# Direct products issued by high and low terms, each with its own wait, in an order planned from the engines' first moments

## The chip, the cores and the metric

The kernel runs on one core of a Trainium2 chip. The core has a matrix engine (PE in the profile, with its weight loads shown apart as PEld), two engines for elementwise work (DVE and ACT), a fourth that is hardly used here (POOL), and queues that issue DMA transfers (SP's, and a few on ACT). The metric is the device time of one launch in microseconds. Of the kernel before, three runs gave 1079.13, 1081.22 and 1082.68 us.

## The reference, cut to what matters

```
# attention in chunks of 32 queries; window 16 left, 8 right, and 8 memory slots
scores = 0.125 * q_c @ k_full.T ; a = softmax(scores) ; out = a @ v_full
x = out, as 3072 tokens x 512
# first expert layer
h = x @ w_in ; r = max(h, 0) ; g = s * r*r + b ; x1 = g @ w_out       # 512 -> 2048 -> 512
# second expert layer
h = x1 @ w_in2 ; g = h * sigmoid(1.702 * h) ; y = g @ w_out2
```

All inputs and the output are float32. (The weights w_in and w_out reach the kernel as raw 64-bit words, which it turns into float32 itself.)

## The kernel before, in words

**Two ways of multiplying.** Every operand of a large product is split into a high and a low part (a float32r value, and the rest), and three terms are computed: high times high, high weight times low data, low weight times high data. In the trace the parts of weights are `wih`/`wil` (w_in) and `woh`/`wol` (w_out), those of the tokens `xh`/`xl`, those of the gated middle layer `gh`/`gl`. The first four of the six blocks of 512 tokens go through the first layer as *direct products* (`step`, lines 630 to 632 and 668): `ph` is one 128-row slice of h, and `accA`, `accB` gather the four slices of the result. All the rest, from about 438 us on, are products of a Winograd-like scheme with seven pieces (`wino`, lines 998 to 1004 and 1153): there one sum is copied by ACT from one PSUM bank to another (line 1046), and further products are added onto the copy.

**Units.** A unit of direct work is one slice of 128 of the 2048 middle features, for a block of 512 tokens: 12 matmuls into `ph` (4 slices of the model width, 3 terms), then relu, square, scale and shift, then a cast to `gh` and a subtraction to `gl`, then 12 matmuls into `accA` and `accB`. The first two slices are done in two halves of 256 tokens (A: tiles 0 and 1; Z: tiles 2 and 3), so that direct work can begin before the whole block has been through the attention.

**Attention.** Tiles of 128 tokens, singly for tiles 0 to 3 and then in pairs. PE computes the scores `sc` (line 441), DVE the maximum and the subtraction, ACT the exponent (line 466), PE turns the result (`pp`, line 474), ACT or DVE copy it (`px`), PE multiplies with the values (`o`, line 502), DVE divides (line 507), PE turns it back (`xx`, line 516), and ACT or DVE cast `xh` (line 238) and DVE subtracts `xl` (line 533). The buffers for keys, queries and values hold two tiles, so the loads for tiles 2 and 3 are issued when the work on tiles 0 and 1 has let go of them. Weights are read by DMA into `st`, put together by two ACT and three DVE instructions, and split.

**The planner.** The order of everything is fixed when the program is built. Each piece of work is an operation of class `Plan` with a time by which it is wanted, the engines that could do it with a duration for each, and what it waits for. `order` places the operations one by one: the earliest start wins, among near ones the earliest due; a DMA ends a constant after its bytes have passed a single shared pipe; an operation on another engine is ready 0.15 us after what it waits for. All engines begin at time 0. A DMA's constant is 1.0 us for issues up to 12 us and 2.2 us later. Each engine then executes its list strictly in that order; an instruction that is not ready holds up all behind it.

**Fillers.** Where the plan leaves PE without work for more than 0.3 us before the fourth operation of `plan.first` (the first accumulating products), it puts in matmuls on a tile of zeros (`idle<-cold`, line 1291), one for every 0.24 us of the gap, and ten more at the very start (`warm<-cold`, line 288). Each float32 filler is two passes in the trace.

**What the change touches.** `WARM`; the constants of `Plan`, the line with the free times in `order`, and the two lines that turn gaps into fillers; in `step` the functions `hid` (four operations of 3 matmuls, all of which wait for every high and low part) and `out_part` (four operations of 3 matmuls, all of which wait for `gh`, `gl`, `woh` and `wol`), and the operations made of them.

Of the kernel before, what the change touches and what calls it, by code (L numbers as in the profile page):

```python
# [32 lines left out]
WARM = 10  # L33
# [15 lines left out]
class Plan:  # L49


    DMA_START, DMA_END, DMA_LATER = 1.1, 1.0, 2.2
    BEAT = 0.24

# [19 lines left out]
    def order(self):  # L74
# [7 lines left out]
        free = {"pe": 0.0, "act": 0.0, "dve": 0.0, "pool": 0.0, "sp": 0.0, "aq": 0.0, "none": 0.0}  # L82
# [53 lines left out]
        while left:  # L136
# [29 lines left out]
            if e in ("sp", "aq"):  # L166
# [5 lines left out]
                ends[i] = dma_free + (self.DMA_LATER if t > 12.0 else self.DMA_END)  # L172
# [32 lines left out]
def attention_moe_moe(ctx: ExitStack, tc: tile.TileContext, q_t, k_w, v_w, w_in1, w_out1, s_b, w_in2, w_out2, out):  # L205
# [409 lines left out]
    def step(i):  # L615
# [7 lines left out]
        def hid(k):  # L623
            def fn(e):
                if k == 0:
                    T["ph", i] = ps_h.tile([P, 512], F32, tag="h", name="ph")[:, :r.stop - r.start]
                wh, wl = [w[:, k * P:(k + 1) * P] for w in T[win]]
                xh, xl = [x[:, k, r] for x in T["x", m, b]]
                ph = T["ph", i]
# [28 lines left out]
        def out_part(k):  # L658
            def fn(e):
                if fresh and k % 2 == 0:  # L660
                    T["acc", group, k // 2] = pair(halves[k // 2], halves[k // 2])
                a = T["acc", group, k // 2][:, k % 2]
                wh, wl = T[wout]
                gh, gl = T["g", i]
                s = slice(k * P, k * P + P)
                terms = ((a[:, r], wh[:, s], gh), (a[:, r], wh[:, s], gl), (a[:, r], wl[:, s], gh))
                for x, (o, lt, rh) in enumerate(terms):
                    nc.tensor.matmul(o, lt, rh, start=fresh and x == 0, stop=(done and x == 2))  # L668
            return fn

        dur = 0.68 * n + (0.0 if n == 1 else 0.03)
        d = None
        uses = [("h", i)]
        ready = list(o_w[win])
        for x in {0: range(2), 256: range(2, 4)}[r.start] if r != ALL else range(4):
            ready += o_x[4 * b + x]
# [673 lines left out]
```

## Time and profile before

| | |
|---|---|
| runs | 1081.22 us (median of 1079.13, 1081.22, 1082.68) |
| profiled execution | 1080.21 us, of which the span from first to last instruction is 1078.2 us |
| PE | 1061.2 us busy, 8653 matmuls |
| DVE, ACT | 760.0 us and 603.8 us busy |
| DMA | 265.68 MB, 246 GB/s on average |

A row of a timeline gives the start and the length of a piece of work in us, the engine, the source line, the operation, what it writes and reads, its shape, how many instructions were merged into the row, and in brackets how long the engine had been idle and what ended that. The ends of matmuls are modelled and overlap the next one's start, so times between matmuls are read from start to start: a matmul of 128x512 takes 0.39 us by its length, and the next one starts 0.23 us after it.

### The profile page before, as it was taken

To read this page: it belongs to the slowest core of one execution; us is meant where nothing else is said; L and a number is where in the kernel's file an instruction comes from. 1 tells how busy PE (TensorE), PEld (TensorE's weight loads), DVE (VectorE), ACT (ScalarE), POOL (GpSimd) and SP (SyncE) were. 2 spreads that over 40 slices of the span, in tenths; PEclk is the share of its full clock that TensorE was granted. 3 is DMA by queue.
4 is the path that set the end of the run, shared out by engine and by line. 5 is a ranking of instruction groups with operands and counts; after the bars stand their busy time and mean duration, and the time that the engine had idled before them with its cause. 6 is when DMAs were issued, how large, how long until landed. Compare 5 with 4: busy or idle time off the path is not lost.

```text
span 1078.2 us, 21826 instructions
## 1 busy us (share of the span) xinstructions
PE 1061.2 (98%) x8653; PEld 915.4 (85%) x8653; DVE 760.0 (70%) x1146; ACT 603.8 (56%) x929; POOL 0.7 (0%) x6
## 2 busy tenths in 40 slices
PE   8999999999999999999999999999999999999998
PEld 8878888888888788777888787999888999888998
DVE  6899895777888678878899466995224985222954
ACT  4777755555666566678744566553455542454432
POOL 0000000000000000000000000000000000000000
PEclk9999999999999999999999999999999999999999
DMA  9898843667699985979878889867666766656662
GB/s 349 284 321 292 263 136 129 230 210 233 226 344 330 318 292 186 314 247 312 305 220 295 299 304 334 301 221 254 195 190 201 235 207 213 196 188 207 196 199 79
DMA packets 151541, 265.68 MB, mean 246 GB/s; under 512 B 14224, under 2 KB 65424, under 8 KB 151440
## 3 DMA queue, kind: packets, MB, share of 16 engines
q1 hardware_dynamic: 151152, 263.77, 73.7%
q8 instruction: 68, 1.11, 0.4%
q10 hardware_dynamic: 288, 0.52, 0.1%
q14 instruction: 33, 0.27, 0.1%
HBM read 190.84 MB, written 73.40 MB: 245 GB/s over the span
## 4 chain that ended last, share of the span: by engine, by line
PE 94%; DMA 2%; ACT 2%; DVE 1%; issue 1%; DVEq 0%; SPq 0%; ACTq 0%
PE pc L1153 10%; PE accA L668 8%; PE accB L668 7%; PE pd L1153 6%; PE pb L1153 6%; PE ph L630 6%; PE ph L632 5%; PE ph L631 5%; PE pc L1159 3%; PE pd L1002 3%; PE pd L1004 3%; PE pd L1003 3%; PE ph L1002 3%; PE ph L1003 3%; PE ph L1004 3%; PE pb L1002 2%
## 5 line engine op out<-in xcount | busy, mean ns | idle before, releaser
L1127 DVE TENSOR_TENSOR oj<-G,oj 128x1024 fp32r<-128x1024 f32 x72 | 87.9, 1223 | 54.4 <-ACT oj L1124 53.7
L1124 ACT CAST oj<-G 128x1024 fp32r<-128x1024 f32 x72 | 75.6, 1051 | 87.7 <-PE pd L1153 28.9
L637 ACT ACTIVATE r<-ph 128x512 f32<-128x512 f32 (+1 forms) x66 | 38.6, 585 | 68.9 <-PE ph L632 60.0
L1124 ACT CAST oq<-G 128x1024 fp32r<-128x1024 f32 x40 | 42.1, 1052 | 48.2 <-PE pc L1153 20.0
L1127 DVE TENSOR_TENSOR oq<-G,oq 128x1024 fp32r<-128x1024 f32 x40 | 48.9, 1223 | 27.8 <-ACT oq L1124 27.6
L1153 PE MATMUL pc<-wih,oj 128*128 128x256 f32 x336 | 62.4, 283 | 0.0
L1136 DVE TENSOR_TENSOR G<-G 128x1024 f32<-128x1024 f32 x48 | 57.4, 1219 | 0.2
L652 ACT CAST gh<-r 128x512 fp32r<-128x512 f32 (+1 forms) x66 | 40.1, 607 | 31.3 <-PE accB L668 27.0
L656 DVE TENSOR_TENSOR gl<-r,gh 128x512 fp32r<-128x512 f32 (+1 forms) x66 | 44.2, 669 | 18.1 <-ACT gh L652 17.8
L1014 ACT ACTIVATE G<-ys 128x512 f32<-128x512 f32 x64 | 40.5, 633 | 24.0 <-DVE ys L1056 24.0
L630 PE MATMUL ph<-xh,wih 128*128 128x512 f32 (+1 forms) x136 | 53.8, 396 | 0.0
L1153 PE MATMUL pd<-wih,oj 128*128 128x256 f32 x288 | 53.8, 283 | 0.0
L1153 PEld LDWEIGHTS pc<-wih,oj 128*128 128x128 f32 x336 | 53.3, 192 | 0.0
L631 PE MATMUL ph<-xl,wih 128*128 128x512 f32 (+1 forms) x136 | 52.2, 384 | 0.3 <-DVE xl L533 0.3
L632 PE MATMUL ph<-xh,wil 128*128 128x512 f32 (+1 forms) x136 | 52.0, 383 | 0.3 <-DVE wil L333 0.3
L668 PE MATMUL accA<-gl,woh 128*128 128x512 f32 (+1 forms) x132 | 51.1, 387 | 1.0 <-DVE gl L656 1.0
L668 PE MATMUL accA<-gh,woh 128*128 128x512 f32 (+1 forms) x132 | 51.3, 389 | 0.0
L668 PE MATMUL accB<-gh,woh 128*128 128x512 f32 (+1 forms) x132 | 51.1, 387 | 0.0
L668 PE MATMUL accA<-gh,wol 128*128 128x512 f32 (+1 forms) x132 | 50.7, 384 | 0.0
L668 PE MATMUL accB<-gl,woh 128*128 128x512 f32 (+1 forms) x132 | 50.5, 383 | 0.2 <-issue 0.2
L355 ACT ACTIVATE u<-st 128x512 f32<-128x512 f32 x64 | 43.0, 673 | 13.7 <-DMA st<-w_in 11.0
L668 PE MATMUL accB<-gh,wol 128*128 128x512 f32 (+1 forms) x132 | 50.6, 383 | 0.0
(253 smaller groups left out, 3111.3 us busy)
## 6 DMA issues: line engine op xcount, KB each, us to landing
wih<-wodh SPq DMA_DIRECT2D x112, 256.0 KB, 3.2
wil<-wodl SPq DMA_DIRECT2D x112, 256.0 KB, 3.7
wih<-wch SPq DMA_DIRECT2D x96, 256.0 KB, 3.7
wil<-wcl SPq DMA_DIRECT2D x96, 256.0 KB, 4.0
st<-w_in SPq DMA_DIRECT2D x32, 512.0 KB, 5.6
st<-w_out SPq DMA_DIRECT2D x32, 512.0 KB, 5.9
k<-k_w SPq DMA_DIRECT2D x24, 512.0 KB, 6.5
v<-v_w SPq DMA_DIRECT2D x24, 512.0 KB, 6.1
```

What stands on the lines that cost most here:

```text
L630: nc.tensor.matmul(ph, wh, xh, start=(k == 0), stop=False)
L631: nc.tensor.matmul(ph, wh, xl, start=False, stop=False)
L632: nc.tensor.matmul(ph, wl, xh, start=False, stop=(k == KT - 1))
L656: nc.vector.tensor_tensor(out=gl, in0=T["r", i], in1=gh.bitcast(F32), op=ALU.subtract)
L668: nc.tensor.matmul(o, lt, rh, start=fresh and x == 0, stop=(done and x == 2))
L1002: nc.tensor.matmul(ph, wh, xh, start=first and i == 0, stop=False, skip_group_check=True)
L1003: nc.tensor.matmul(ph, wh, xl, start=False, stop=False, skip_group_check=True)
L1004: nc.tensor.matmul(ph, wl, xh, start=False, stop=i == 1, skip_group_check=True)
L1124: nc.scalar.copy(out=T[kh], in_=g_of(ty, z))
L1127: nc.vector.tensor_tensor(out=T[kl], in0=g_of(ty, z), in1=T[kh].bitcast(F32), op=ALU.subtract)
L1136: o_raw[out, x] = [op(need, {"dve": 1.22}, lambda e: nc.vector.tensor_tensor(out=g_of(out, z), in0=g_of(a, z), in1=g_of(b, z), op=o), afte ...
L1153: nc.tensor.matmul(a, lt[:, z], rh, start=first and t % 2 == 0 and x == 0, stop=p == HALF - 1 and x == 2, skip_group_check=True)
```

## The change

It replaces the four operations of three terms by three operations of one term each: for `ph` first high times high for all four slices of the width, which waits only for the high weight and the high tokens; then high weight times low tokens, waiting for the low tokens; then low weight times high tokens, waiting for the low weight. The planner may put either of the last two first, and other work between them. The products into `accA` and `accB` are split likewise (high times `gh`, which waits for `gh` and `woh`; then those with `gl` and with `wol`), except in the last unit of a block, which stays as it was. The number and the shapes of the matmuls are the same.

The planner's engines now begin at 0.7 to 1.0 us, each DMA ends 2.2 us after its bytes, a gap becomes fillers only for what is over 0.3 us of it, the warming matmuls are 8, and the fillers end at the first accumulating operation, not at the fourth.

```diff
-WARM = 10
+WARM = 8
...
-    DMA_START, DMA_END, DMA_LATER = 1.1, 1.0, 2.2
+    DMA_START, DMA_END = 1.1, 2.2
     BEAT = 0.24
+    BEGIN = {"pe": 1.0, "act": 0.7, "dve": 0.8, "pool": 0.7, "sp": 0.7, "aq": 0.7, "none": 0.0}
...
-        free = {"pe": 0.0, "act": 0.0, "dve": 0.0, "pool": 0.0, "sp": 0.0, "aq": 0.0, "none": 0.0}
+        free = dict(self.BEGIN)
...
-                ends[i] = dma_free + (self.DMA_LATER if t > 12.0 else self.DMA_END)
+                ends[i] = dma_free + self.DMA_END
...
                 if idle > 0.3:
-                    full.append((None, int(idle / self.BEAT)))
+                    full.append((None, int((idle - 0.3) / self.BEAT)))
...
-        def hid(k):
-            def fn(e):
-                if k == 0:
+        def hid(x, y):
+            def fn(e):
+                if not seen_["hid"]:
                     T["ph", i] = ps_h.tile([P, 512], F32, tag="h", name="ph")[:, :r.stop - r.start]
...
-                nc.tensor.matmul(ph, wh, xh, start=(k == 0), stop=False)
-                nc.tensor.matmul(ph, wh, xl, start=False, stop=False)
-                nc.tensor.matmul(ph, wl, xh, start=False, stop=(k == KT - 1))
+                for k in range(KT):
+                    seen_["hid"] += 1
+                    nc.tensor.matmul(T["ph", i], T[win][x][:, k * P:(k + 1) * P], T["x", m, b][y][:, k, r],
+                                     start=seen_["hid"] == 1, stop=seen_["hid"] == 3 * KT)
...
-        for k in range(KT):
-            after = list(ready)
-            if d is not None:
-                after.append(d)
-            d = op(at_h[i], {"pe": dur}, hid(k), after=after, alloc=[("h", ("h", i))] if k == 0 else [],
-                   uses=[("x", m, b), win])
+        wh, wl = o_w[win]
+        high, low = [x[0] for x in tokens], [x[1] for x in tokens]
+        d = op(at_h[i], {"pe": third}, hid(0, 0), after=[wh] + high, alloc=[("h", ("h", i))], uses=[("x", m, b), win])
+        ds = [op(at_h[i], {"pe": third}, hid(0, 1), after=[d] + low, uses=[("x", m, b), win]),
+              op(at_h[i], {"pe": third}, hid(1, 0), after=[d, wl], uses=[("x", m, b), win])]
...
-            if fresh and not plan.first[3:]:
-                plan.first.append(d)
...
+        if done:
+            ds = []
+            for k in range(KT):
+                ds.append(op(at_o[i], {"pe": dur}, out_part((k,), ((0, 0), (0, 1), (1, 0))), after=[g1, g2, wh, wl] + prev + ds[-1:],
...
+        else:
+            d = op(at_o[i], {"pe": third}, out_part(range(KT), ((0, 0),)), after=[g1, wh] + prev, alloc=taken, uses=[("g", i), wout])
+            ds = [op(at_o[i], {"pe": third}, out_part(range(KT), ((0, 1),)), after=[d, g2], uses=[("g", i), wout]),
+                  op(at_o[i], {"pe": third}, out_part(range(KT), ((1, 0),)), after=[d, wl], uses=[("g", i), wout])]
+            if fresh and not plan.first:
+                plan.first += [d]
```

The plan made from this differs from the plan before over the first half of the program; the last 2665 matmuls stand in the same order. (Line numbers of the changed kernel are higher by one, and `ph` and the accumulators have one line each, 632 and 665.) Three places on PE:

**The way to the first direct product.** PE before, from the attention of tiles 0 and 1 to the first direct product of half A. Ahead of these rows stand 1 filler, 10 warming matmuls, the scores of tile 0, 9 fillers, the scores of tile 1 and the first turn.

```order
L1291 MATMUL idle<-cold 128x128 x3
L502 MATMUL o<-v,px 32x64 x32
L1291 MATMUL idle<-cold 128x128 x8
L474 MATMUL pp<-ident,qe 128x128 x4
L516 MATMUL xx<-ident,px 128x128 x4
L1291 MATMUL idle<-cold 128x128
L502 MATMUL o<-v,px 32x64 x32
L1291 MATMUL idle<-cold 128x128 x6
L516 MATMUL xx<-ident,px 128x128 x4
L1291 MATMUL idle<-cold 128x128 x9
L630 MATMUL ph<-xh_351,wih 128x256
L631 MATMUL ph<-xl_352,wih 128x256
```

The same place now. Ahead of it stand 3 fillers, 8 warming matmuls, 5 fillers, the scores of tile 0, 10 fillers, the scores of tile 1 and the first turn.

```order
L1292 MATMUL idle<-cold 128x128 x2
L503 MATMUL o<-v,px 32x64 x32
L1292 MATMUL idle<-cold 128x128 x5
L475 MATMUL pp<-ident,qe 128x128 x4
L517 MATMUL xx<-ident,px 128x128 x4
L503 MATMUL o<-v,px 32x64 x32
L1292 MATMUL idle<-cold 128x128 x4
L517 MATMUL xx<-ident,px 128x128 x4
L1292 MATMUL idle<-cold 128x128 x2
L632 MATMUL ph<-xh_353,wih 128x256 x4
L632 MATMUL ph<-xh_353,wil 128x256 x4
L632 MATMUL ph<-xl_354,wih 128x256 x4
```

From the scores of tile 0 to the first direct product stand 36 fillers before and 23 now, and ahead of those scores 11 fillers and warming matmuls before and 16 now; the four products with the low tokens come last.

**The last pair of attention tiles.** PE before, from the scores of the last pair of tiles on; `ph` belongs to a unit of the fourth block.

```order
L441 MATMUL sc<-k,qe 32x64 x64
L630 MATMUL ph<-xh_3311,wih 128x512
L631 MATMUL ph<-xl_3312,wih 128x512
L632 MATMUL ph<-xh_3311,wil 128x512
L630 MATMUL ph<-xh_3311,wih 128x512
L631 MATMUL ph<-xl_3312,wih 128x512
L632 MATMUL ph<-xh_3311,wil 128x512
L630 MATMUL ph<-xh_3311,wih 128x512
L631 MATMUL ph<-xl_3312,wih 128x512
L632 MATMUL ph<-xh_3311,wil 128x512
L630 MATMUL ph<-xh_3311,wih 128x512
L631 MATMUL ph<-xl_3312,wih 128x512
```

PE now, from the same scores on.

```order
L442 MATMUL sc<-k,qe 32x64 x64
L632 MATMUL ph<-xh_3313,wih 128x512 x4
L665 MATMUL accA<-gh,woh 128x512 x2
L665 MATMUL accB<-gh,woh 128x512 x2
L665 MATMUL accA<-gl,woh 128x512 x2
L665 MATMUL accB<-gl,woh 128x512 x2
L665 MATMUL accA<-gh,wol 128x512 x2
L665 MATMUL accB<-gh,wol 128x512 x2
L665 MATMUL accA<-gh,woh 128x512 x2
L665 MATMUL accB<-gh,woh 128x512 x2
L665 MATMUL accA<-gl,woh 128x512 x2
L665 MATMUL accB<-gl,woh 128x512 x2
```

The turn `pp` of that pair came after 12 matmuls of 128x512; now 48 of them stand between the scores and it.

**A product onto a copied sum.** PE before, some 40 us into the Winograd part: the last of the products A of a piece into `ph`, and those that follow into the bank `pb`, whose other half takes ACT's copy of that sum.

```order
L1003 MATMUL ph<-xh_5202,wih 128x512
L1004 MATMUL ph<-xh_5202,wil 128x512
L1002 MATMUL pb<-xl_5508,wih 128x512
L1003 MATMUL pb<-xl_5508,wih 128x512
L1004 MATMUL pb<-xl_5508,wil 128x512
L1002 MATMUL pb<-xl_5508,wih 128x512
L1003 MATMUL pb<-xl_5508,wih 128x512
L1004 MATMUL pb<-xl_5508,wil 128x512
```

PE now, after the same products into `ph`.

```order
L1004 MATMUL ph<-xh_5199,wih 128x512
L1005 MATMUL ph<-xh_5199,wil 128x512
L1003 MATMUL pc<-wzh,wih 128x512
L1004 MATMUL pc<-wzl,wih 128x512
L1005 MATMUL pc<-wzh,wil 128x512
L1003 MATMUL pc<-wzh,wih 128x512
L1004 MATMUL pc<-wzl,wih 128x512
L1005 MATMUL pc<-wzh,wil 128x512
L1003 MATMUL pd<-wzh,wih 128x512
L1004 MATMUL pd<-wzl,wih 128x512
```

Twelve other products (into `pc` and `pd`) now stand between the sum and the first product into `pb`. At two more places of that part, where `pd` followed twelve products into `pc` at once, six products into `pd` from other operands now stand in between.

On ACT, at the passage from direct to Winograd products, the copies of the four finished sums (`y<-accA` twice, `y<-accB` twice) and one cast `sx<-sx` of 128x1024 now stand ahead of the cast of `xh` that the second group of Winograd products waits for; before, DVE did that cast, after one such copy.

## Rows read from the trace of the kernel before

**Rows 1.** The page: PE's busy time, and the chain that ended last.

```profile
PE 1061.2 (98%) x8653; PEld 915.4 (85%) x8653; DVE 760.0 (70%) x1146; ACT 603.8 (56%) x929; POOL 0.7 (0%) x6
...
PE 94%; DMA 2%; ACT 2%; DVE 1%; issue 1%; DVEq 0%; SPq 0%; ACTq 0%
```

**Rows 2.** Waits of PE: who waited for whom; us in total, times, longest.

```profile
PE xx L516 <- DVE px L507: 1.5, 1, 1.5
PE pd L1002 <- ACT pd L1046: 1.3, 2, 0.7
```

**Rows 3.** Busy time by stretch: PE, PEld, DVE, ACT, POOL (instructions); PEclk; DMA.

```profile
36.00:39.00 3.00, 2.94 (x14) 2.95 (x15) 2.99 (x7) 0.76 (x2) 0.00 (x0) 0.50 0.95 285
39.40:42.40 3.00, 3.00 (x28) 3.00 (x27) 2.35 (x6) 2.85 (x7) 0.00 (x0) 1.00 0.72 200
442.10:445.50 3.40, 3.40 (x9) 2.68 (x9) 3.40 (x8) 1.14 (x3) 0.00 (x0) 0.50 0.90 288
60.00:100.00 40.00, 39.13 (x539) 31.10 (x538) 36.03 (x63) 32.09 (x56) 0.00 (x0) 1.00 0.91 325
```

**Rows 4.** Timeline of PE, 0 to 43 us.

```profile
1.64 4.10 PE L288 MATMUL warm<-cold 128*128 128x128 f32 x20
5.67 0.86 PE L441 MATMUL sc<-k,qe 64*32 64x64 f32 x64
6.46 2.27 PE L1291 MATMUL idle<-cold 128*128 128x128 f32 x18
...
12.40 0.42 PE L502 MATMUL o<-v,px 64*32 64x64 f32 x21 [0.71 <-issue]
...
20.87 0.36 PE L630 MATMUL ph<-xh,wih 128*128 128x256 f32 x1
...
25.13 0.63 PE L441 MATMUL sc<-k,qe 64*32 64x64 f32 x36 [0.85 <-issue]
...
34.02 0.63 PE L516 MATMUL xx<-ident,px 128*128 128x128 f32 x4 [1.48 <-DVE px L507]
...
36.06 0.58 PE L631 MATMUL ph<-xl,wih 128*128 128x256 f32 x1 [0.31 <-DVE xl L533]
...
42.51 0.40 PE L630 MATMUL ph<-xh,wih 128*128 128x512 f32 x1
```

**Rows 5.** Timeline of DVE around 33 us.

```profile
32.58 0.69 DVE L238 CAST xh<-xx 128x512 fp32r<-128x512 f32 x1 [0.56 <-PE xx L516]
33.19 0.68 DVE L507 TENSOR_TENSOR px<-o,den 128x512 f32<-128x512 f32 x1
```

**Rows 6.** DMA issues from 15.2 to 16.2 us: KB each, median us to landing.

```profile
qe<-q_t SPq DMA_DIRECT2D x2, 256.0 KB, 6.2
```

**Rows 7.** Timeline of PE around the last pair of attention tiles.

```profile
357.88 1.51 PE L441 MATMUL sc<-k,qe 64*32 64x64 f32 x128
...
363.30 0.88 PE L474 MATMUL pp<-ident,qe 128*128 128x128 f32 x6 [0.97 <-ACT qe L466]
...
369.73 0.50 PE L668 MATMUL accA<-gl,woh 128*128 128x512 f32 x1 [0.72 <-DVE gl L656]
```

**Rows 8.** Timeline of PE at a product onto a copied sum.

```profile
479.52 0.39 PE L1004 MATMUL ph<-xh,wil 128*128 128x512 f32 x1
480.57 0.50 PE L1002 MATMUL pb<-xl,wih 128*128 128x512 f32 x1 [0.66 <-ACT pb L1046]
```

**Rows 9.** Timeline of PE at the passage to Winograd products.

```profile
438.31 0.39 PE L668 MATMUL accB<-gh,wol 128*128 128x512 f32 x1
440.88 0.50 PE L1002 MATMUL ph<-xh,wih 128*128 128x512 f32 x1 [1.27 <-DVE xh L238]
441.82 0.57 PE L1003 MATMUL ph<-xh,wih 128*128 128x512 f32 x1 [0.43 <-DVE xh L901]
```

**Rows 10.** Timeline of ACT at the same passage.

```profile
437.38 1.07 ACT L238 COPY y<-accA 128x512 f32<-128x512 f32 x2 [3.46 <-PE accA L668]
...
439.34 1.06 ACT L830 CAST sx<-sx 128x1024 fp32r<-128x1024 f32 x1
```

More of the change, by code (lines that the diff above doesn't have):

```diff
@@ L656, in gate4, with out_part @@
             nc.vector.tensor_tensor(out=gl, in0=T["r", i], in1=gh.bitcast(F32), op=ALU.subtract)
-        def out_part(k):
+        def out_part(ks, terms):
             def fn(e):
[L660 to L668, printed above, removed]
+                for k in ks:
+                    if fresh and k % 2 == 0 and ("acc", group, k // 2) not in T:
+                        T["acc", group, k // 2] = pair(halves[k // 2], halves[k // 2])
+                    for x, y in terms:
+                        nc.tensor.matmul(T["acc", group, k // 2][:, k % 2][:, r], T[wout][x][:, k * P:k * P + P], T["g", i][y],
+                                         start=fresh and (x, y) == (0, 0), stop=done and (x, y) == (1, 0))
@@ L669, in out_part @@
             return fn
         dur = 0.68 * n + (0.0 if n == 1 else 0.03)
-        d = None
+        third = dur * KT / 3
         uses = [("h", i)]
-        ready = list(o_w[win])
-        for x in {0: range(2), 256: range(2, 4)}[r.start] if r != ALL else range(4):
-            ready += o_x[4 * b + x]
-        for k in range(KT):
-            after = list(ready)
-            if d is not None:
-                after.append(d)
-            d = op(at_h[i], {"pe": dur}, hid(k), after=after, alloc=[("h", ("h", i))] if k == 0 else [],
-                   uses=[("x", m, b), win])
+        tokens = [o_x[4 * b + x] for x in ({0: range(2), 256: range(2, 4)}[r.start] if r != ALL else range(4))]
@@ L683, in step @@
+        wh, wl = o_w[win]
[3 more added lines that the diff above has]
+              op(at_h[i], {"pe": third}, hid(1, 0), after=[d, wl], uses=[("x", m, b), win])]
         need = at_o[i] - 0.6
-        d = op(need, {"act": 0.18 + 0.42 * n}, gate1, after=[d, o_sb], alloc=[("r", ("r", i))], uses=uses)
+        d = op(need, {"act": 0.18 + 0.42 * n}, gate1, after=ds + [o_sb], alloc=[("r", ("r", i))], uses=uses)
@@ L688, in step @@
         g2 = op(need, {"dve": 0.12 + 0.54 * n}, gate4, after=[g1], uses=[("r", i)])
[L689 to L698 removed]
+        wh, wl = o_w[wout]
+        taken = [(halves[x], ("acc", group, x)) for x in range(2)] if fresh else []
+        prev = o_y.get(group, [])
+        if done:
+            ds = []
+            for k in range(KT):
+                ds.append(op(at_o[i], {"pe": dur}, out_part((k,), ((0, 0), (0, 1), (1, 0))), after=[g1, g2, wh, wl] + prev + ds[-1:],
+                             alloc=[x for x in taken if not k % 2 and x[1][2] == k // 2], uses=[("g", i), wout]))
+                finish(m, b, k, group, lo, hi, ds[-1], at_o[i] + 4)
+        else:
[4 more added lines that the diff above has]
+                plan.first += [d]
+        o_y[group] = [d] + ds if not done else ds
     o_store = {}
```

12 lines of the change are left out of this document (1 added, 11 removed).

## The prediction, made before the changed kernel ran

> **What bounds the kernel now.** I read the page first. PE is busy for 98% of the span and makes up 94% of the chain that ended last [rows 1], so time is won only where PE stands still, runs filler, or runs at the lower clock. The number of matmuls does not change, so nothing is won in the work itself. Second, the waits of PE; [rows 2] are the two longest for which this change matters. Third, the stretches: behind the start the granted clock was 0.50, that is 1.2 of 2.4 GHz, in two alone, around 36 to 39 us and 442 to 445 us; 3 us of the first hold 14 matmuls, and 3 us right after it 28 of the same kind [rows 3]. Each lasts about 3.4 us, at half the rate, so it costs 1.7 us. Fourth, the timelines at these places [rows 4, 7 to 9].
>
> So four places can move: the start up to the first 512-wide direct product at 42.51 us [rows 4], the last attention pair at 358 us, the passage to the Winograd part at 439 us, and the products that wait for a copied sum.
>
> **The start: -3.5 us.** Step by step.
>
> (a) Ahead of the first scores, 11 fillers and warming matmuls became 16. A filler is two passes. The warming ones cost (5.67 - 1.64) / 20 = 0.20 us a pass, at the lower rate; the 18 passes behind the first scores cost 2.27 / 18 = 0.126 us each [rows 4]. The first scores started the moment the warming ended, so five more calls, ten passes at the later rate, put them 1.2 us later: about 6.9 us.
>
> (b) From there to the first direct product 36 fillers became 23: 13 calls, 26 passes at 0.126, is 3.3 us. If the data came in time, that product would start at 20.87 + 1.2 - 3.3 = 18.8 us. It won't quite: behind the last turn `xx` the cast of `xh` must still be done, and with only two fillers left this cast, not filler, is late next. I take 19.4 us; 1.5 us are won. The low tokens are the last to be cast, and the new order asks for them last, behind four products with the low weight.
>
> (c) Next come the scores of tiles 2 and 3. Their queries were issued at 15.3 to 15.7 us and take 6.2 us to land, in a stretch in which transfers queue up [rows 6]. They are there at about 21.5 to 21.9 us whatever PE does. So these scores can't run from 20.5 us. With two times 0.8 us and the stop of 0.85 us in their middle, which nothing in the profile explains and which I keep, they end at about 24.2 us, against 25.13 + 0.63 = 25.8 us [rows 4]: still 1.5 us won.
>
> (d) Then the maxima, exponents and turns follow as before, 1.5 us earlier. Before, DVE put a cast of `xh` between the divisions of tile 2 and of tile 3 [rows 5], and the last turn `xx` waited 1.48 us for the second [rows 4]. Now the two divisions stand side by side. What is late next is ACT's cast of both `xh`, behind the turns. I count 1.3 of these 1.5 us: 2.8 us won so far.
>
> (e) The direct product of half Z waited 0.31 us for `xl` [rows 4]; it now has eight products with the high tokens to do first: 3.1 us.
>
> (f) The lower clock at 36 us came 1.5 us after the stop of 1.48 us; stops of 0.71 and 0.85 us earlier brought none [rows 3, 4]. The largest gaps that I find in the new order are about half a microsecond. So I take this stretch of 1.7 us as gone: 4.8 us.
>
> (g) One thing is put off: the scores of tile 4 (0.8 us) stood before 42.51 us and stand behind now. And 128 products `o` of tiles 2 and 3 now follow each other directly, like the scores that stopped for 0.85 us; I charge half of that. 4.8 - 0.8 - 0.4 = 3.6, and I write 3.5 us. The bounds: 1.5 us, if the clock falls again and that stop comes in full; 4.8 us, if the clock holds and neither stop comes.
>
> **The last attention pair: -1.7 us.** Between its scores and its turn stood 12 matmuls (2.7 us), while maximum, subtraction and exponent took from 359.4 to 363.3 us; PE waited 0.97 us, and the same delay made a `gl` 0.72 us late [rows 7]. Now 48 matmuls, 10.9 us, stand between. The wait goes; the second is a matter of DVE's order there, so between 0 and -1.7 us. I take all of it, since both are rows of one queue.
>
> **Products onto a copied sum: -2.4 us.** From the last product A at 479.52 us to the first product onto its copy at 480.57 us are 1.05 us instead of 0.23, so such a place costs 0.8 us [rows 8]. Three of them (this one, and the two of `pd` [rows 2]) have 6 or 12 other products, 1.4 or 2.7 us, in between now, more than the copy needs. The other such places stand as they were. Bounds: 0, if ACT comes to the copies later in its new order, to -2.4.
>
> **The passage: +0.7 us.** Direct work ends at 438.54 us; the second Winograd group waited for the cast `xh` until 440.88 and for its low part until 441.82 us, and the clock fell [rows 9]. Now ACT does that cast, behind four copies of some 0.5 us and the cast `sx` of 1.06 us [rows 10]; and DVE does the low part of that `sx`, about as long, ahead of that of `xh`. Counted from the end of direct work the cast is then ready at +2.5 us (+2.3 before), the low part at +3.9 (+3.3). The fall of the clock stays. +0.7, between -1 and +2.
>
> **The rest of the order: +1.2 us.** DVE is busy 36.0 of 40 us from 60 to 100 us [rows 3], so a PE that comes 3.5 us earlier finds weights and `gl` ready only if DVE is earlier too. It is, since its own waits at the start were for PE; the spare 4 us cover the rest only if they fall right. Besides, all of the order up to the last 2665 matmuls was dealt anew, and the deal before brought stops like those of [rows 2, 7]. No row shows it: between 0 and the whole 3.5 us of the start. I take a third.
>
> **Sum.** -3.5 - 1.7 - 2.4 + 0.7 + 1.2 = -5.7 us. From the profiled execution (span 1078.2 us, 2.0 us around it, 1080.21 us) this gives 1074.5 us; the median of the runs shown lies 1.0 us above that execution, so 1075.5 us.
>
> **A rule against it.** The two falls of the clock came behind stops of 1.48 us and of 1.27 and 0.43 us; behind 0.66 us at 479.5 us none came, since the low clock stands in two stretches alone [rows 3, 8, 9]. The Trainium skill, TensorE: Matmul & The Clock Gate, in "A second HAM failure mode: psum-queue depth-cycling", says that short idle times between groups of matmuls, often enough, make the clock swing between its two levels. This kernel has fewer fillers and more waits, so by that rule it would be the third rival below; the trace so far speaks for stops of over a microsecond only.
>
> **The rivals.**
>
> *First, what is won at the start is given back to DVE and the transfers.* For it: queries that land at 21.5 us [rows 6] and DVE at 90% from 60 to 100 us [rows 3]. Against it: DVE's waits at the start are for PE. The +1.2 becomes +3.5, and if ACT comes late to half of the copies as well, 1081.2 - 5.7 + 2.3 + 1.2 = 1079 us. 0.20.
>
> *Second, the change doesn't do what it says.* The planner's clock is shifted and its lists are dealt anew, but new stops take the place of the old: 1.5 and 1.3 us of [rows 2] and 1.7 us of [rows 7] come back elsewhere, 1081.2 - 5.7 + 4.5 = 1080 us, give or take 3. For it: PE's stops were placed by the same rules; against it: those of [rows 7, 8] have 1.4 to 10.9 us of other work in their place. 0.12.
>
> *Third, slower: the clock.* PE stands still more often, for about half a microsecond, between 1 and 45 us, since fillers end one operation earlier and are fewer. If the clock falls there, each fall costs 1.7 us [rows 3], and DVE's and PE's chains of the first 45 us are strung behind each other, so none of it is hidden. The fall at 36 us staying takes 1.7 us of the gain; from the fourth further fall on the kernel is slower than before, and with six, 1081.2 - 5.7 + 7 x 1.7 = 1087 us. For it: fewer fillers; against it: stops of 0.71 and 0.85 us brought no fall. 0.06.
>
> **How the numbers follow.** The forecast, 1072 to 1078 us, has 0.62, the first rival 0.20, the second 0.12, the third 0.06. What a measurement can tell from no change is about 0.3%, 3.2 us: faster means below 1078.0 us. The forecast lies there, and a third of the first rival: 0.62 + 0.06 = 0.68. Same: most of the rest of the first two, 0.24. Slower: the third and a little of the second, 0.08. The range from 1071 to 1081.5 us leaves out the third rival and the ends of the second.
>
> **What would show it.** Right: the first direct product between 19 and 20 us, the first 512-wide one before 40 us, no stretch at 0.50 before 50 us and one at about 440 us; no wait of `pp` for the last pair, none of `pd` for ACT's copies. Wrong: a low clock between 30 and 45 us; new waits of PE on DVE from 60 to 110 us; a stop of more than 2 us at the passage, or copies on ACT that come late.

## The result, and the profile after

The change made the kernel slower, by half a percent. Before: median 1080.31 us (1078.52 to 1082.68, 7 runs); after: 1086.42 us (1083.84 to 1088.74, 7 runs). The ratio is 1.0053, 95% interval 1.0035 to 1.0070. The forecast was 1075.5 us, with a range from 1071 to 1081.5. The profiled execution after took 1083.84 us, 3.6 more than that of before, and is the fastest of its seven runs; the rest of the difference of medians (2.5 us) is in executions without a trace.

Page and waits of PE in the kernel after, against [rows 1, 2]:

```profile
PE 1057.8 (98%) x8645; PEld 915.0 (85%) x8645; DVE 757.7 (70%) x1136; ACT 605.0 (56%) x939; POOL 0.7 (0%) x6
q8 instruction: 68, 1.11, 0.4%
PE 91%; DVE 1%; ACT 1%; DMA 1%; issue 1%; DVEq 0%; SPq 0%
```

```profile
PE sc L442 <- issue: 7.3, 4, 4.6
PE ph L632 <- DVE wih L239: 3.5, 2, 2.4
PE ph L1003 <- ACT xh L239: 1.3, 1, 1.3
PE ph L632 <- ACT wih L239: 1.2, 1, 1.2
```

The waits of [rows 2] are gone. The scores now stop for 7.3 us in all, and what the profile names is "issue", that is no other engine; products wait 4.7 us (3.5 + 1.2) for casts of weights. The start and one later burst of small matmuls, timeline of PE after, against [rows 4]:

```profile
18.98 0.38 PE L1292 MATMUL idle<-cold 128*128 128x128 f32 x1 [0.50 <-issue]
19.12 0.72 PE L632 MATMUL ph<-xh,wih 128*128 128x256 f32 x4
...
21.34 1.38 PE L442 MATMUL sc<-k,qe 64*32 64x64 f32 x110
27.28 0.63 PE L442 MATMUL sc<-k,qe 64*32 64x64 f32 x18 [4.56 <-issue]
...
37.59 0.74 PE L632 MATMUL ph<-xh,wih 128*128 128x256 f32 x4 [0.23 <-ACT xh L239]
...
43.44 1.09 PE L632 MATMUL ph<-xh,wih 128*128 128x512 f32 x4
...
68.07 1.20 PE L632 MATMUL ph<-xh,wih 128*128 128x512 f32 x4 [1.07 <-DVE wih L239]
77.63 1.20 PE L632 MATMUL ph<-xh,wih 128*128 128x512 f32 x4 [1.19 <-ACT wih L239]
91.08 1.19 PE L632 MATMUL ph<-xh,wih 128*128 128x512 f32 x4 [2.44 <-DVE wih L239]
...
198.44 1.48 PE L442 MATMUL sc<-k,qe 64*32 64x64 f32 x126 [0.21 <-issue]
201.97 0.27 PE L442 MATMUL sc<-k,qe 64*32 64x64 f32 x2 [2.05 <-issue]
```

The stretches at the two long stops, and one at the passage to Winograd products (busy time; the clock is the column behind POOL), against [rows 3]:

```profile
25.00:31.70 6.70, 4.42 (x36) 4.25 (x37) 3.18 (x7) 1.23 (x2) 0.00 (x0) 0.50 0.64 220
202.50:205.70 3.20, 3.20 (x9) 2.43 (x8) 3.17 (x6) 0.00 (x0) 0.00 (x0) 0.50 0.78 266
445.00:452.00 7.00, 4.77 (x19) 3.05 (x17) 4.07 (x6) 6.03 (x11) 0.00 (x0) 1.00 1.07 382
```

The clock falls to 0.50 (1.2 of 2.4 GHz) at both stops: in the trace's clock records from 24.91 us, in the middle of the first, for 6.83 us, and from 202.40 us, behind the second, for 3.41 us. It no longer falls at 36 or 442 us.

How far TensorE lies behind the kernel before at the same point of the work (from the matmul records of both traces: the work done is counted with each shape of matmul at its usual distance from start to start, fillers left out; minus is ahead). The columns are the times of the kernel before:

| us | 21 | 27 | 38 | 65 | 96 | 186 | 207 | 348 | 371 | 517 | 691 to the end |
|---|---|---|---|---|---|---|---|---|---|---|---|
| after | -1.8 | +3.2 | +2.4 | +1.1 | +4.9 | +4.9 | +9.0 | +9.7 | +7.4 | +4.9 | +3.8 |
| after, run again (e12) | +1.0 | +2.4 | +0.9 | -0.4 | +3.1 | +3.1 | +7.4 | +8.1 | +5.8 | +3.2 | +2.2 |
| terms only (e1) | -0.4 | -1.1 | -1.5 | -1.3 | +2.0 | +1.8 | +1.9 | +2.4 | +0.5 | -1.0 | -2.0 |
| terms, weights 4 us earlier (e7) | -1.6 | -0.8 | -1.5 | -1.3 | -0.7 | -0.9 | -0.6 | +0.1 | -2.1 | -4.6 | -5.7 |
| after, late 64 places (e16) | -0.4 | +3.8 | +2.6 | +1.3 | +6.9 | +7.4 | +7.3 | +11.5 | +9.1 | +6.6 | +5.5 |

So the loss has three places: 21 to 27 us, 65 to 96 us, and 200 us.

### The profile page after: what moved, and what is told of

Its sections match the earlier page's. It is cut to its first block, busy times and chain, and to the rows that moved or that the text cites. A ratio compares the mean times of both kernels' runs of the same rounds, so it can differ in the third digit from the quotient of the medians.

```text
span 1082.1 us, 21815 instructions
## 1 busy us (share of the span) xinstructions
PE 1057.8 (98%) x8645; PEld 915.0 (85%) x8645; DVE 757.7 (70%) x1136; ACT 605.0 (56%) x939; POOL 0.7 (0%) x6
## 4 chain that ended last, share of the span: by engine, by line
PE 91%; DVE 1%; ACT 1%; DMA 1%; issue 1%; DVEq 0%; SPq 0%
PE ph L632 15%; PE pc L1154 10%; PE accA L665 7%; PE accB L665 7%; PE pd L1154 6%; PE pb L1154 6%; PE pc L1160 3%; PE ph L1003 3%; PE pd L1003 3%; PE pd L1005 3%; PE ph L1005 3%; PE ph L1004 3%; PE pd L1004 3%; PE pc L1003 2%; PE pb L1003 2%; PE pb L1005 2%
## 5 line engine op out<-in xcount | busy, mean ns | idle before, releaser
L1154 PE MATMUL pc<-wil,oj 128*128 128x256 f32 x168 | 47.6, 283 | 0.0
L1154 PEld LDWEIGHTS pd<-wih,oj 128*128 128x128 f32 x288 | 45.8, 192 | 0.0
L1154 PE MATMUL pc<-wih,oq 128*128 128x256 f32 x240 | 45.6, 283 | 0.0
L368 DVE SCALAR_TENSOR_TENSOR u<-u,st 128x512 uint32<-128x512 uint32 x64 | 43.2, 684 | 2.6 <-ACT st L364 1.6
L1154 PE MATMUL pb<-wih,oj 128*128 128x256 f32 x240 | 44.7, 283 | 0.0
L374 DVE SCALAR_TENSOR_TENSOR u<-st,u 128x512 uint32<-128x512 uint32 x64 | 43.0, 683 | 0.2
L364 ACT ACTIVATE st<-st 128x512 uint32<-128x512 uint32 x64 | 43.0, 676 | 0.0
L632 PE MATMUL ph<-xh,wih 128*128 128x512 f32 (+1 forms) x136 | 37.6, 399 | 4.9 <-DVE wih L239 3.5
L645 ACT ACTIVATE r<-r 128x512 f32<-128x512 f32 (+1 forms) x66 | 40.8, 619 | 1.2
```

The source lines that it names most:

```text
L364: nc.scalar.activation(out=lo, in_=lo, func=AF.Copy, scale=7.49 * 2.0**-32)
L368: nc.vector.scalar_tensor_tensor(out=u, in0=u, scalar=3, in1=T["st", i][:, :, 0], op0=ALU.logical_shift_left, op1=ALU.bitwise_or)
L632: nc.tensor.matmul(T["ph", i], T[win][x][:, k * P:(k + 1) * P], T["x", m, b][y][:, k, r], start=seen_["hid"] == 1, stop=seen_["hid"] == 3 ...
L1154: nc.tensor.matmul(a, lt[:, z], rh, start=first and t % 2 == 0 and x == 0, stop=p == HALF - 1 and x == 2, skip_group_check=True)
```

## The experiments

**Theory A: the stops are fetches of TensorE's own instructions.** Queue q8 moved 68 packets of 16 KB, one for each 256 of PE's 17,540 instructions in this kernel (8645 weight loads, as many matmuls, and 250 others, most of them waits). Counted from the start, every longer stop that "issue" ends in the first 30 us lies at instruction 256 k + 193: 449, 705 and 961 (the last matmul ahead of them starts at 11.47, - and 24.06 us before, and at 12.03, 18.21 and 22.50 us after), and at 200 us it is 4545. I call such a place a boundary. The packet that 961 waits for, its fetch, began at 24.82 us, when PE had stood for 2.3 us, and PE went on 1.4 us behind the packet's end. (A bracket gives the time that PE was idle; from start to start such a stop is some 0.2 us longer.) In the 20 traces 63 stops of over 0.6 us lie at such a place, and in every one PE goes on 1.2 to 1.6 us behind the end of a packet on q8. DMA of the kernel after, 17.6 to 24.6 us (first row) and 24.6 to 26 us (queue, kind: packets, MB, share):

```profile
q1 hardware_dynamic: 987, 2.64, 103.6%
...
q8 instruction: 1, 0.02, 4.7%
```

No data were missing: the queries had landed at 21.87 us. At 200 us the DMA engines hardly moved data (199.4 to 200.7 us):

```profile
q8 instruction: 1, 0.02, 4.9%
q1 hardware_dynamic: 2, 0.00, 1.5%
```

There the fetch began 1.7 us after PE had passed the boundary before, the packet took 1.0 us, and PE went on 1.4 us behind it: 4.1 us for a block of 256, which the burst had used up in 1.9 us. The stop of 2.3 us is the difference.

The Trainium skill, Runtime: NRT & Kernel Launch, "Instruction fetch mechanics", says that an engine's instructions come in blocks of 16 KiB, 256 instructions, over a queue of its own, ahead of need and mostly hidden. The trace agrees on size and queue (68 packets of 16 KB on q8), and not on hidden (4.8 us for 961 and 2.3 us for 4545, from start to start). The rivals of theory A for the stops are late data and the throttle of the clock. For the rest of the loss two more theories stand: C, that VectorE's order makes the weights late, and P, that the planner's new constants do the harm.

**e1, the terms alone; e2, the constants alone.** e1 is the kernel after with the planner's old first moments, transfer times and filler rule and ten warming matmuls; e2 is the kernel before with the new ones and eight (and the old products). Two lines of e1's edit; e2's is the reverse:

```diff
-    DMA_START, DMA_END = 1.1, 2.2
+    DMA_START, DMA_END, DMA_LATER = 1.1, 1.0, 2.2
...
-        free = dict(self.BEGIN)
+        free = {"pe": 0.0, "act": 0.0, "dve": 0.0, "pool": 0.0, "sp": 0.0, "aq": 0.0, "none": 0.0}
```

> The change's products by terms, with the planner's old first moments, transfer times, fillers and warm-up. Theory A (TensorE stops where a new block of 256 of its instructions has not been fetched in time, and loses its clock there): the time follows the place of those blocks, not the edit, so a stop over 1.5 us among scores or values is there or not by where a block boundary falls; the terms themselves are worth what the prediction gave them after 40 us, about 4 us (three stops of about 0.8 us at copied sums, 1.7 us at the last attention pair), so 1074 to 1078 without such a stop and 1080 to 1084 with one. Theory C (the terms let the planner place VectorE and ScalarE work ahead of the weight casts, and TensorE waits for the casts from 60 to 92 us): 1083 to 1087, with the three waits for wih of 1 us and more at 60 to 92 us again. Theory P (the new constants do the harm): 1075 to 1079.

> The kernel before with the change's planner constants, first moments, fillers and warm-up, but products by column block with one wait. Theory A: again by the place of the blocks, 1078 to 1086; if a stop over 1.5 us shows, it starts at a multiple of 256 TensorE instructions plus 193. Theory C: no waits for wih over 1 us at 60 to 92 us, 1078 to 1081. Theory P (the constants do the harm): 1083 to 1088.

e1: 1078.49 us, ratio 0.9975 (0.9958 to 0.9993); e2: 1082.92 us, 1.0025 (1.0001 to 1.0049). One gains 0.25%, the other loses it, and together they lose 0.53%, so they don't add. In e2 (a profiled execution of 1088.32 us, 5.4 us above its median) the same stop, PE:

```profile
24.79 1.31 PE L442 MATMUL sc<-k,qe 64*32 64x64 f32 x104
29.53 0.43 PE L442 MATMUL sc<-k,qe 64*32 64x64 f32 x24 [3.44 <-issue]
```

In e1 the burst runs through:

```profile
24.14 1.51 PE L441 MATMUL sc<-k,qe 64*32 64x64 f32 x128
```

With the old constants PE takes 5.1 us from the end of the stop at 705 to instruction 961 (before and e1), with the new ones 3.5 us (after; 3.9 us in e2). P is right for the start. From 65 to 96 us both parts lose: e1 loses 3.3 us, of which 1.8 us are a wait for an exponential at 87.4 us, and e2's trace has a stop of 3.15 us ahead of the scores at 89.32 us and a fall of the clock from 88.94 us. The profile calls that stop "issue" too, but it lies at no boundary and ends 0.1 us behind VectorE's `xl`: the word alone does not make a stop a fetch.

**e3, e4: every instruction 128 or 64 places later.**

```diff
-        for _ in range(WARM):
+        for _ in range(WARM - 2):
...
+        for _ in range(34):
+            nc.tensor.matmul(w[:32, :64], T["cold"][:64, :32], T["cold"][:64, :64], start=True, stop=True)
```

> The changed kernel with two of its eight warming matmuls replaced by 34 small ones, so that every later TensorE instruction stands 128 places later and nothing else changes. Theory A: the stop of 2.3 us at 199.7 us and the clock's fall behind it go (4 us), and the stop of 4.8 us at 27 us changes its place and falls below 2 us (3 to 5 us with its fall of the clock): 1077 to 1082. Its rivals (the stop is a wait for the keys and queries, or the throttle's own doing, or the order of VectorE's work): nothing changes, 1085 to 1088, with the stops where they were.

> The same with one warming matmul replaced by 17 small ones, 64 places. Theory A: the stop at 199.7 us goes with its fall of the clock (4 us); the one at 27 us may keep 1 to 4 us, since the third block is asked for only 1 us earlier: 1079 to 1084. Its rivals: 1085 to 1088, the stops where they were.

e3: 1088.95 us, 1.0067 (1.0041 to 1.0094); e4: 1084.90 us, 1.0020 (0.9998 to 1.0043). The stops at 961 and 4545 are gone in both, so they hang on the count, which speaks against the throttle. Against late data speaks, for 961, that the queries had landed, and for 4545 e16 below, which moves nothing else. The times were missed. The small matmuls took 4.0 and 3.8 us and put the first scores 3.9 and 5.4 us later, and e3 got a new stop at 2497 = 256 x 9 + 193, PE:

```profile
65.62 1.29 PE L444 MATMUL sc<-k,qe 64*32 64x64 f32 x103
69.72 0.66 PE L444 MATMUL sc<-k,qe 64*32 64x64 f32 x25 [2.81 <-issue]
```

**e5: shorter data queue.** Two loads of `v` are moved in SP's list behind the next weight loads:

```diff
+        moved = [x for x in order if x[0] in plan.moved]
+        order = [x for x in order if x[0] not in plan.moved]
+        spot_ = [x[0] for x in order].index(plan.front)
+        order[spot_:spot_] = moved
```

> The changed kernel with the two loads of v for tiles 2 and 3 issued by SP four entries later, behind the next weight loads and stores, all else in its order. Theory A (the stop of 4.8 us at 27 us is a fetch of TensorE's instructions that stands behind data transfers): the fetch that started at 24.8 us starts at 20 to 22 us, the stop at the 961st instruction is under 2 us, the clock doesn't fall at 25 us, and TensorE is 3 to 6 us ahead of the changed kernel at 35 us; the stop at 199.7 us stays where it was unless the order of waits shifts it, so 1079 to 1084. If the stop was a wait for keys and queries or the throttle's own: unchanged at 27 us, 1085 to 1089.

1085.70 us, 1.0050 (1.0036 to 1.0065): a miss. The stop is 2.7 us (2.9 from start to start), and the clock falls for 3.41 instead of 6.83 us, but the fetch came at 24.34 us although the DMA engines stood still from 22.0 to 22.5 us. Counted from PE's passing 705 that is 3.8 us instead of 5.8. So a queue of data isn't all of the delay. Whether it is a part of it is not shown: e12 below, with nothing moved, has 3.7 us.

**e6 to e8: weights due earlier.** On the kernel after (e6, 4 us) and on e1 (e7, 4 us; e8, 6 us):

```diff
+        for i in self.rush:
+            late[i] -= self.RUSH
```

> The changed kernel with the planner's due times of the first pass's weights, from the fourth block on, 4 us earlier, so that VectorE's ninth decoded block comes nearer to where it stands before. Theory C (VectorE's and ScalarE's order lets the weights come late from 60 to 92 us): the three waits for wih fall from 4.7 us to under 2 us, 1082 to 1085 with the stop at 27 us left as it is. Theory A alone: 1085 to 1088.

> The products by terms on the planner's old constants (the first experiment), with the weights' due times 4 us earlier. Theory C: the 3.3 us lost from 60 to 95 us in the first experiment come back in most part: 1074 to 1077. If the weights are bound by their decoding and transfers and not by the order: 1078 to 1080. Theory A: a stop over 2 us may come up anywhere that bursts of small matmuls meet a block's boundary, and then 1080 to 1083.

> The same with 6 us. Theory C: 1074 to 1077, or 1077 to 1080 if the attention, which then comes later, becomes what TensorE waits for from 65 to 95 us.

e6: 1094.19 us, 1.0134 (1.0118 to 1.0149): a miss. The waits for weight casts fell from 4.7 to 2.2 us, but at 208 us PE waited 3.9 us for an exponential, and the clock fell there. e7: 1077.28 us, 0.9970 (0.9954 to 0.9985), **faster than both kernels**: from 65 to 96 us it loses 0.6 us where e1 lost 3.3, and no stop is over 1.33 us. (Its trace, of 1074.32 us, is 3 us below its median and has no fall of the clock but at the very end.) e8: 1084.59 us, 1.0038 (1.0025 to 1.0052), a miss, with stops of 3.24 us at 449 and about 3 us at 2753. The order of its first 30 us on PE is e7's; only the fetch for 449 came later (12.60 us for 9.92). So the place of a stop is set, and its size differs between executions.

**e9: 112 places later, by small fillers in place of four large ones.**

```diff
-            for _ in range(e):
+            nth += 1
+            for _ in range(e - 4 if nth == 3 else e):
...
+            for x in range(32 if nth == 3 else 0):
+                z, c = slice(64 * (x % 2), 64 * (x % 2) + 64), slice(32 * (x // 2 % 4), 32 * (x // 2 % 4) + 32)
+                nc.tensor.matmul(idle[c, x % 2, :64], T["cold"][z, c], T["cold"][z, :64], start=True, stop=True)
```

> The changed kernel with 4 of the 10 filler matmuls at 7 us replaced by 32 small ones laid out as the scores are (about 0.9 us for 1.0), so that every later TensorE instruction stands 112 places later without the 4 to 6 us that the two earlier shifts cost at the start. The boundary that fell behind the first half of the burst at 21 to 23 us then falls in its middle, and the one before it 256 instructions earlier, at about 15.5 us, so TensorE takes over 6 us from one to the next. Theory A (a block's fetch that comes later than TensorE reaches it): no stop over 1 us at 22 to 28 us and none at 196 to 203 us, no fall of the clock at either, and, if VectorE's lost time is what returns at 60 to 92 us (theory D: VectorE bounds that stretch, and what it loses at the stop TensorE pays there), also the waits for wih shrink: 1076 to 1080. Theory A without D: 1079 to 1083. Rivals (data, throttle): 1085 to 1088.

1085.85 us, 1.0061 (1.0038 to 1.0085): a miss on the time. Both stops went, and others came at 449 and 2497, each with a fall of the clock for 6.83 us, PE:

```profile
10.07 0.73 PE L442 MATMUL sc<-k,qe 64*32 64x64 f32 x50
13.47 0.46 PE L442 MATMUL sc<-k,qe 64*32 64x64 f32 x14 [2.68 <-issue]
...
66.02 1.36 PE L442 MATMUL sc<-k,qe 64*32 64x64 f32 x111
70.28 0.35 PE L442 MATMUL sc<-k,qe 64*32 64x64 f32 x17 [2.91 <-issue]
```

**e10, e11: VectorE relieved** (theory D, that it owes PE at 60 to 92 us what it lost at the stop): no clamp of the first pass's weights, on the kernels after and before.

```diff
-            nc.vector.tensor_scalar(out=uf, in0=uf, scalar1=2.0, scalar2=1.875 * 2.0**32, op0=ALU.max, op1=ALU.min)
+            if m:
+                nc.vector.tensor_scalar(out=uf, in0=uf, scalar1=2.0, scalar2=1.875 * 2.0**32, op0=ALU.max, op1=ALU.min)
```

> The changed kernel without the clamp of the first pass's 32 weight blocks on VectorE (0.43 us each; this part of the computation is left out), about 17 of them before 92 us. Theory D (VectorE bounds 36 to 92 us and pays there for the stop at 27 us): the three waits for wih, 4.7 us, fall to under 1.5 us, the stops at 27 and 200 us stay: 1081 to 1084. If transfers bound that stretch: the waits stay, 1085 to 1088.

> The kernel before without the same 32 clamps (left out of the computation). Theory D: TensorE waits there for VectorE's work less than 1 us from 48 to 100 us, so 0 to 1.5 us are gained: 1079 to 1081. If it gains 3 us or more, VectorE's work bounds the kernel before in another place.

e10: 1083.36 us, 1.0031 (1.0015 to 1.0048); e11: 1078.65 us, 0.9996 (0.9977 to 1.0016), no gain that can be told from none. The time of e10 fits, the reason doesn't: with some 7 us of VectorE's work left out before 92 us, the waits for weight casts fell from 4.7 to 3.4 us only, and not under 1.5. D falls.

```profile
PE ph L633 <- DVE wih L239: 2.2, 2, 1.5
PE ph L633 <- ACT wih L239: 1.2, 1, 1.2
```

**e12: the kernel after, once more, unchanged.**

> The changed kernel once more, unchanged, for a second look at its places. Theory A: stops at the 961st and the 4545th TensorE instruction again, each within 2 us of its first size (4.8 and 2.3 us), since the places are set by the count and only the fetch's time varies; the clock falls behind both. If the stops were an accident of one execution: they are not there.

One run, 1082.20 us. The places are the same, the sizes are not, PE:

```profile
23.92 1.36 PE L442 MATMUL sc<-k,qe 64*32 64x64 f32 x110
27.79 0.41 PE L442 MATMUL sc<-k,qe 64*32 64x64 f32 x18 [2.51 <-issue]
...
196.62 1.48 PE L442 MATMUL sc<-k,qe 64*32 64x64 f32 x126 [0.21 <-issue]
200.42 0.27 PE L442 MATMUL sc<-k,qe 64*32 64x64 f32 x2 [2.33 <-issue]
```

The clock fell behind the second, not behind the first, which is also just over 2 us shorter than in the first trace: on both points the expectation was missed.

**e13, e14: SP's order.** The weight load of 78.8 us goes ahead of four entries, in the kernel after and in e1:

```diff
+        back = [x for x in range(at) if order[x][1] == "sp"][-4:]
+        order[at + 1:at + 1] = [order[x] for x in back]
+        for x in back[::-1]:
+            del order[x]
```

> The changed kernel with one entry of SP's queue moved: the weight load that was issued at 78.8 us goes ahead of the two loads of v and the two stores of casts that stood before it; nothing else moves. Theory E (SP's order: the load's buffer was free at 75.6 us, but SP waited for the values' matmuls and two casts first, and the weight came 3 us late): it is issued at 75.5 to 76.5 us, TensorE's wait of 2.4 us for wih at 91 us falls under 0.8 us, the two earlier waits (1.1 and 1.2 us) stay: 1083 to 1085. Theory D (VectorE's debt): the wait stays and the time too, 1085 to 1088.

> The products by terms on the old constants with the same load moved ahead of the same four entries (it was issued at 76.9 us, its buffer free at 72.3). Theory E: it is issued at 72.5 to 74 us, the wait of 1.8 us for the exponential at 87.4 us and the 0.3 us behind it go, 1075.5 to 1077.5. Theory D: 1078 to 1080.

e13: 1085.46 us, 1.0036 (1.0020 to 1.0052); e14: 1077.99 us, 0.9980 (0.9960 to 1.0000). In e13 the load landed in 4.3 us instead of 7.5, but the last wait for `wih` was still 1.7 us (2.4 in the kernel after), and in e14 that for the exponential was 1.93 us. Both are misses; theory E alone falls. e13's stop at 961 was the longest, 7.2 us from start to start.

**e15: wide fillers**, up to 512 columns in one matmul:

```diff
-            for _ in range(e):
-                nc.tensor.matmul(idle[:, 0, :P], T["cold"], T["cold"], start=True, stop=True)
+            for x in range(0, e, 4):
+                c = P * min(4, e - x)
+                nc.tensor.matmul(idle[:, 0, :c], T["cold"][:, :P], T["cold"][:, :c], start=True, stop=True)
```

> The changed kernel with its filler and warming matmuls up to 512 columns wide, so that 14 calls stand where 49 stood before the scores of tiles 2 and 3: the same TensorE time, 140 instructions fewer. Theory A: the 705th instruction falls into the burst at 22 us and the 961st into the values at 30 us, far enough apart: no stop over 1.5 us at 22 to 28 us and no fall of the clock there, 2 to 4 us ahead of the changed kernel at 35 us; the stop at 200 us goes too, but each shift so far has brought one elsewhere: 1078 to 1084. If stops come from transfers or the throttle alone: 1085 to 1088 with the stop at 27 us.

1083.11 us, 1.0028 (1.0007 to 1.0049), as expected of A. (In the traces 14 filler and warming matmuls stand ahead of the scores of tiles 2 and 3 where 41 stood, not 49, so 108 instructions fewer.) At the start there is no long stop, and the scores wait for what step (c) had named, the queries; TensorE is 4.1 us ahead at 54 us. It has lost all of it and more by 96 us: a stop comes at 1985, the clock falls behind it and again from 89.85 us, and the waits for casts are still there. One more stop, of 1.8 us, comes at 7105 (307 us). PE:

```profile
22.11 1.55 PE L443 MATMUL sc<-k,qe 64*32 64x64 f32 x128 [0.96 <-DMA qe<-q_t]
...
57.75 1.03 PE L518 MATMUL xx<-ident,px 128*128 128x128 f32 x8 [2.21 <-issue]
```

**e16 to e18.** e16 shifts the count by 64 places at 142 us only. e17 has SP's move of e13 and, on VectorE, one maximum behind the weight's cast. e18 has both. The matmuls of e16, and e17's move on VectorE:

```diff
+                    for w in range(16 if i == 20 else 0):
+                        c = slice(32 * (w % 4), 32 * (w % 4) + 32)
+                        nc.tensor.matmul(T["ph", i][c, :64], ident[:64, c], ident[:64, :64], start=True, stop=True)
...
+        here = [x for x, _ in order].index(plan.casts[14])
+        back = [x for x in range(here) if order[x][0] in plan.tops][-1]
+        order.insert(here + 1, order[back])
+        del order[back]
```

> The changed kernel with 16 small matmuls (64 instructions, 0.4 to 0.9 us, into a product's bank that the product then overwrites) at about 142 us, in the stretch of products only, so that nothing before it changes and every instruction behind it stands 64 places later. Theory A: the stop of 2.3 us at 200 us and the clock's fall behind it go (4.0 us), one of about 1 us may come at 315 us as in the run with 64 places from the start: 1082.5 to 1084.5. Rivals of A (the throttle's own, or the scores' data): the stop stays and the pad's time is added, 1086 to 1088.

> The changed kernel with two moves: the weight load ahead of four SP entries as in the run before, and on VectorE the maximum of the next scores (1.1 us) behind the cast of that weight instead of ahead of it. Theory F (each in-order queue holds the weight a little: SP, then VectorE): TensorE's last wait for wih, 2.4 us, falls under 0.8 us, and the exponential that hangs on the maximum is not waited for: 1.3 to 2 us gained, 1084 to 1085. If VectorE's whole work is the limit there: the wait goes over to the next weight or the next softmax in the same size, 1085 to 1088.

> The changed kernel with the late 64 places and both moves. Theories A and F: 1080.5 to 1083.5, what is left over the kernel before being the start and the first two waits for casts. If A alone holds: 1082.5 to 1084.5; if neither: 1085 to 1088.

e16: 1084.32 us, 1.0032 (1.0017 to 1.0048), as expected of A. The burst at 200 us runs through, and the clock stays there; from 186 to 207 us nothing is lost where the kernel after lost 4.0 us. At 316 and 348 us stops of 1.3 and 1.2 us come instead, at 7617 and 8385. (From 65 to 96 us its trace lost more than that of the kernel after: a fall of the clock from 92.83 us came on top.) PE:

```profile
201.22 1.50 PE L442 MATMUL sc<-k,qe 64*32 64x64 f32 x128 [0.21 <-issue]
...
317.46 0.30 PE L442 MATMUL sc<-k,qe 64*32 64x64 f32 x3 [1.29 <-issue]
...
349.40 0.50 PE L635 MATMUL ph<-xh,wil 128*128 128x512 f32 x1 [1.22 <-issue]
```

e17: 1084.79 us, 1.0036 (1.0020 to 1.0053). The last wait fell from 2.4 to 1.05 us, and the one before it grew from 1.2 to 1.6: F holds in part. PE:

```profile
78.44 1.19 PE L635 MATMUL ph<-xh,wih 128*128 128x512 f32 x4 [1.60 <-ACT wih L239]
90.54 1.20 PE L635 MATMUL ph<-xh,wih 128*128 128x512 f32 x4 [1.05 <-DVE wih L239]
```

e18: 1084.64 us, 1.0031 (1.0013 to 1.0048), a miss: the two did not add. A stop at 961 of 5.0 us and falls of the clock from 29.5 and 449.3 us stand in its trace.

## Why the prediction was wrong

Two steps failed: (c) of the start, and the term for the rest of the order.

**Step (c)** kept the stop in the scores at its 0.85 us [rows 4] as something that no row explained. Steps (a) and (b) came as forecast (first scores at 6.42 us for 6.9, first direct product at 19.12 for 19.4), but the stop grew from 1.1 to 4.8 us from start to start. Some 1.6 us of that come from PE, which reaches instruction 961 only 3.5 us behind the stop at 705, not 5.1; some 2 us come from the fetch, which began at 24.82 us, where that of before began at 22.85. Why it began later stays open. The stop was 2.7, 2.7, 2.9, 4.3, 4.8, 4.8, 5.0, 5.9 and 7.2 us in the nine traces whose start has the new order (after, e5, e6, e10, e12, e13, e16, e17, e18), 3.7 us in e2, and at most 1.4 us in the six with the old order (before, e1, e7, e8, e11, e14). The scores were over at 27.84 us instead of 24.2, with the clock at 0.50 until 31.74 us.

**(d) to (f) were right and came too late.** The turns `xx` no longer wait for a division, half Z does not wait for `xl`, and the clock doesn't fall at 36 us. How much of that last gain is the change's is not shown: e11, the kernel before without its clamps, has the stop of 1.47 us at 34 us and no fall. (The clock records put the fall of before at 35.93 us, 1.9 us behind that stop's end; (f) read 1.5.) The first 512-wide product still came at 43.44 us, not at 39.0. Up to 65 us the start gives +1.1 us for the -3.5 forecast.

**The rest of the order: +1.2 was mis-sized; +8.6 measured** in the two traces compared: 3.9 us from 65 to 96 us, 4.0 at 200 us, 0.7 from 207 to 348 us. The 4.0 us are one stop of 2.3 us at a boundary and a clock fall's 1.7, for which the prediction had no term; e16 shows it. The 3.9 us go with the waits for casts (4.7 us). Of their causes only a part is shown: the order of SP and VectorE makes half of the last one (e17, though 0.4 us came back in the wait before). Earlier due times took 2.5 us off those waits in the kernel after and cost more elsewhere (e6); in e1, whose loss there is mostly another wait, they remove most of it (e7). What makes the first two waits, 1.1 and 1.2 us in nearly every trace of this order, stays open.

**Right terms.** Last pair: 2.3 us won (forecast 1.7); its turn starts without a wait. Copied sums: 3.1 us won (2.4). Passage: 0.6 us won, where the forecast was a loss of 0.7. The waits there did grow, from the 1.27 and 0.43 us of [rows 9] to 1.33 and 0.85 us, but the clock did not fall; that was luck, since behind the same two waits it fell in the traces of e1, e3, e4, e8 and e18:

```profile
448.47 0.49 PE L1003 MATMUL ph<-xh,wih 128*128 128x512 f32 x1 [1.33 <-ACT xh L239]
449.81 0.50 PE L1004 MATMUL ph<-xh,wih 128*128 128x512 f32 x1 [0.85 <-DVE xh L902]
```

Together: +1.1 + 8.6 - 2.3 - 3.1 - 0.6 = +3.7, for +3.8 in the traces.

**The rivals.** The second (new stops for old) came nearest in kind, at more than its price. The third had the sign, but in this trace the clock fell at stops of 4.8 and 2.3 us, not after many of half a microsecond, so the swing that it feared was not what happened. The first saw the place (VectorE, 60 to 100 us), not the reason: less VectorE work took only 1.3 us off those waits.

## What to carry to other kernels

Count TensorE's instructions before you pull its work forward: where a burst of small matmuls uses up 256 of them in less time than a block took here (4.1 us at 200 us, with the DMA engines nearly idle), the next block's fetch is the limit, and shifting the count moves the stop to another burst (e3, e9, e15, e16). A gain at the start that ends at such a place is no gain. Fewer, wider fillers took the stop at 961 away (e15), though that kernel was not faster in the end. Where two parts of a change can be run apart, run them apart: the terms alone (0.9975) and with earlier weights (0.9970) are faster than the kernel before; with the new constants on top (1.0053) more was lost than either had gained.

## What the runs showed of the hardware that was not expected

- A stop at a block boundary is fixed in place and not in size: 2.7 to 7.2 us at instruction 961 in nine traces. From PE's passing 705 to the start of the fetch for 961 it took 3.7 to 8.4 us in these nine, 3.8 us in e5, whose DMA engines stood still for half a microsecond of it; at 200 us, where the DMA engines were nearly idle in the kernel after, it took 1.6 to 1.7 us in all six traces that have the stop, and that stop was 2.3 to 2.5 us long. What sets the rest is open.
- Stops of like length brought different clocks: 2.51 us at 27 us none, 2.33 us at 200 us a fall (both e12); 1.33 and 0.85 us at the passage none in the kernel after and a fall in e1; the last wait for a cast, of 1.9 to 2.6 us, a fall in e3, e4, e9, e15 and e16 and none in the kernel after, e5 and e12. Each fall before the very end lasted 3.41 or 6.83 us in the clock records.
